# Query-times-kv products in two row tiles of 64 features, over four PSUM banks, and other shares of the banks in each half

## The chip, the cores and the metric

The kernel runs on one core of one Trainium2 chip. The metric is the device time in microseconds (us) of one execution; lower is better. One execution is also recorded by the hardware profiler; all rows below come from it.

The engines are named as in the profile: PE is TensorE (PEld its weight loads), DVE is VectorE, ACT is ScalarE, POOL is GpSimd, SP is the engine that issues most of the DMAs. PE writes to PSUM, which has eight banks of 512 fp32 columns by 128 partitions. Each engine runs its own instructions in order and waits on semaphores for the others.

## The reference

Input x has 2048 rows of 512 features. Two branches work on its normalised form and are added to x:

```python
xn = _layernorm(x, axis=-1)
return x + _A_ref(xn, A_wqkv, A_w_phi, A_wo) + _B_ref(xn, B_w1, B_b1, B_w2)
```

Branch A is linear attention with 32 heads of 16 features. Each head's q and k go through a 16x16 matrix and become two softmaxes of 16, one of p and one of -p:

```python
phi_k = jnp.concatenate([_softmax(pk, axis=-1), _softmax(-pk, axis=-1)], axis=-1)
kv = jnp.einsum("bhsf,bhsd->bhfd", phi_k, v)
z  = jnp.einsum("bhsf->bhf", phi_k)
num = jnp.einsum("bhqf,bhfd->bhqd", phi_q, kv)
den = jnp.einsum("bhqf,bhf->bhq", phi_q, z)[..., None] + 1e-6
o = num / den
```

and o goes through wo. Branch B is a dense layer to 1792 features with bias, Mish, and a dense layer back to 512.

## The kernel before

The 2048 rows are 16 tiles of 128 rows, four tiles to a group. The order of the instructions on every engine is the order in which the code issues them.

**First half** (the loop over s, lines 505 to 542): for each group, project makes logits (p) and values, extremes (DVE) subtracts the largest and smallest of each head, exponentials (ACT) takes Exp, normalise (DVE) divides, and accumulate adds up kv over all rows. Between these, hidden(n) does the next n of 56 units of the dense layer: four matmuls into one PSUM bank (ph), then one Mish on ACT that empties it into acts. Logits and values also go through one bank each, which ACT or DVE empties.

accumulate (line 276) already works in column tiles: its products for 64 features each are put on two halves of PE's columns with tile_position=(0, 64 * r). Its result pkv has eight blocks (two softmaxes pl by four j of eight heads), and mask_kv (line 295) moves them into kvm, keeping only each head's own 16 columns, with the sums z in eight more columns and eight columns of a fixed mask. So a block of kvm is 128 features by 144 columns.

**Second half** (from line 545). exponentials of the query groups 4 to 7 are turned by DMA into qT. attend(h, i) (line 330) multiplies one tile of queries with kvm: eight matmuls of 144 columns, 128 features each, into pnd; four ACT copies move the numerators to nm and the rest to ds. combine(h) (line 359) works for two tiles: DVE makes one divisor out of both softmaxes' sums, multiplies, adds, and a DMA turns the result into oT. second_layer(t) (line 409) opens a bank po and does 14 matmuls of branch B; project_out(h) (line 419) adds four matmuls with wo for each of the tiles 2h and 2h+1, and residual (line 429) adds x on DVE, which empties po, and starts the store.

The loop over h (lines 564 to 590) writes the order out by hand. For h = 1, 3, 4 and 5 it issues combine(h + 1) before project_out(h); for h = 0 and 2 after it, and there four logits follow, and later extremes. Then come attend(h + 2, 0), second_layer(2h + 4), attend(h + 2, 1), second_layer(2h + 5). At h = 5 it issues attend(7, 0), combine(6), combine(7) for its first tile, project_out(5), attend(7, 1) and the second layers of tiles 14 and 15. So when project_out(h) is issued, the po of tiles 2h to 2h + 3 are open. Tile 15 has two po, one for each half of the columns.

**PSUM** is shared out for the whole kernel at the start:

```python
ps = ctx.enter_context(tc.tile_pool(name="ps", bufs=5, space=bass.MemoryType.PSUM))
ps2 = ctx.enter_context(tc.tile_pool(name="ps2", bufs=1, space=bass.MemoryType.PSUM))
```

ps has five banks for all one-bank tiles (pfold, ptr, pproj, ph, po); a new tile takes the bank that has been free the longest, and its first matmul waits until that bank's last reader is done. ps2 is one tile of three banks, which is in turn pwide (three logits at s = 0, lines 516 to 518, emptied by one ACT copy after hidden(6), line 540), pkv and pnd.

Of the kernel before, what the change touches and what calls it, by code (L numbers as in the profile page):

```python
# [1 line left out]

# [15 lines left out]
def kernel(  # L18
# [39 lines left out]
    opool = ctx.enter_context(tc.tile_pool(name="opool", bufs=2))  # L58
    ps = ctx.enter_context(tc.tile_pool(name="ps", bufs=5, space=bass.MemoryType.PSUM))
    ps2 = ctx.enter_context(tc.tile_pool(name="ps2", bufs=1, space=bass.MemoryType.PSUM))  # L60

    x_sb = persist.tile([P, NT, D], BF16, name="x_sb")
    xnT = persist.tile([P, NT, KT, P], BF16, name="xnT")
    acts = persist.tile([P, FT, S], BF16, name="acts")
    kvm = persist.tile([P, 2, 4, 144], BF16, name="kvm")
    wqk = wts.tile([P, KT, 2 * D], BF16, name="wqk")
# [12 lines left out]
    block = consts.tile([P, 8, 16], BF16, name="block")  # L79
    KVmask = consts.tile([P, 136], FP32, name="KVmask")  # L80
    vext = [vpool.tile([P, TPG, 4, 2, 68], BF16, name=f"vext{i}") for i in range(2)]
# [11 lines left out]
    def fold(wT, dst, dve):  # L93

        for kt in range(KT):
            pf = ps.tile([P, 512], FP32, name="pfold", tag="mm")
            for j in range(4):
                nc.tensor.matmul(
                    pf[:, j * P : (j + 1) * P],
                    lhsT=wT[:, j, kt * P : (kt + 1) * P],  # L100
                    rhs=Wbd[:, j, :],
                    start=True,
                    stop=True,
                )
            if kt in dve:
                nc.vector.tensor_copy(dst[:, kt, :], pf[:])
            else:
                nc.scalar.copy(dst[:, kt, :], pf[:])
# [28 lines left out]
    def ln_turn_pe(t, xn, i, copy):  # L137
        ptr = ps.tile([P, 512], BF16, name="ptr", tag="mm")
        for kt in range(KT):
            nc.tensor.transpose(  # L140
                ptr[:, kt * P : (kt + 1) * P], xn[:, i, kt * P : (kt + 1) * P], ident[:]
            )
        copy(xnT[:, t, :, :], ptr[:].rearrange("p (k c) -> p k c", k=KT))
# [7 lines left out]
    def project(w, t, pp=None):  # L151

        if pp is None:
            pp = ps.tile([P, 512], FP32, name="pproj", tag="mm")[:]
        for kt in range(KT):
# [14 lines left out]

    def hidden(n):

        for _ in range(n):
            g, f = next(units)
            ph = ps.tile([P, 512], FP32, name="ph", tag="mm")
            for kt in range(KT):
# [86 lines left out]

    def blocks(kv, pl, j, width):

        bank, at = (pl, j) if j < 3 else (2, pl)
        return kv[:, bank, at * 144 : at * 144 + width]

    def by_parts(kv, c0, c1):

        v = kv[:, :, 0:432].rearrange("p b (k c) -> p b k c", c=144)
        return v[:, 0:2, :, c0:c1], v[:, 2, 0:2, c0:c1]

    kv_of = {}

    def accumulate(g):
        if g == 0:
            kv_of[0] = ps2.tile([P, 3, 512], FP32, name="pkv", tag="kv")
        e = e_of.pop(g)
        for j in range(4):  # L280
            for pl in range(2):
                for i in range(TPG):
                    for r in range(2):
                        c = j * P + 64 * r
                        nc.tensor.matmul(
                            blocks(kv_of[0], pl, j, 65)[64 * r : 64 * r + 64],
                            lhsT=e[:, i, pl, c : c + 64],
                            rhs=vext[g % 2][:, i, j, r, 0:65],
                            start=(g == 0 and i == 0 and (j == 0 or (j == 3 and pl == 0))),
                            stop=(g == NG - 1 and i == TPG - 1),  # L290
# [4 lines left out]
    def mask_kv():  # L295
        for r in range(2):
            rows, c = slice(64 * r, 64 * r + 64), slice(64 * r, 64 * r + 64)
            a, b = by_parts(kv_of[0], 0, 64)
            nc.vector.tensor_tensor(
                out=kvm[rows, :, 0:3, c], in0=a[rows],  # L300
                in1=KVmask[rows, None, None, c].to_broadcast([64, 2, 3, 64]), op=ALU.mult,
            )
            nc.vector.tensor_tensor(
                out=kvm[rows, :, 3, c], in0=b[rows],
                in1=KVmask[rows, None, c].to_broadcast([64, 2, 64]), op=ALU.mult,
            )
        a, b = by_parts(kv_of[0], 64, 65)
        for pl in range(2):
            nc.vector.scalar_tensor_tensor(
                out=kvm[:, pl, 0:3, 128:136], in0=a[:, pl].to_broadcast([P, 3, 8]), scalar=5e-7,  # L310
                in1=KVmask[:, None, 128:136].to_broadcast([P, 3, 8]),
                op0=ALU.add, op1=ALU.mult,
            )
        nc.vector.scalar_tensor_tensor(
            out=kvm[:, :, 3, 128:136], in0=b.to_broadcast([P, 2, 8]), scalar=5e-7,
            in1=KVmask[:, None, 128:136].to_broadcast([P, 2, 8]), op0=ALU.add, op1=ALU.mult,
        )

    def masks():
        nc.gpsimd.memset(kvm[:], 0.0)  # L320
        nc.gpsimd.tensor_copy(KVmask[:, 0:P], block[:].rearrange("p h d -> p (h d)"))
        nc.gpsimd.tensor_copy(KVmask[:, P : P + 8], block[:, :, 0])
        nc.gpsimd.tensor_copy(
            kvm[:].rearrange("p l j c -> p (l j) c")[:, :, 136:144],
            block[:, None, :, 0].to_broadcast([P, 8, 8]),
        )

    nd_of, oT_of, po_of, tmp_of = {}, {}, {}, {}

    def attend(h, i):  # L330

        if i == 0:
            nd_of[h] = (
                (wkp, wv)[h % 2][:].rearrange("p (i l) c -> p i l c", i=2),
                opool.tile([P, 2, 2, 2, 4, 8], FP32, name="ds"),
            )
        nm, ds = nd_of[h]
        pnd = ps2.tile([P, 3, 512], FP32, name="pnd", tag="kv")
        for pl in range(2):
            for j in range(4):  # L340
                nc.tensor.matmul(  # L341
                    blocks(pnd, pl, j, 144),
                    lhsT=qT_of[h][:, i, pl * 4 + j, :],
                    rhs=kvm[:, pl, j, :],
                    start=True,
                    stop=True,
                )
        to = nm[:, i, :, :].rearrange("p l (j c) -> p l j c", j=4)
        a, b = by_parts(pnd, 0, 128)
        nc.scalar.copy(to[:, :, 0:3, :], a)  # L350
        nc.scalar.copy(to[:, :, 3, :], b)
        a, b = by_parts(pnd, 128, 144)
        nc.scalar.copy(
            ds[:, i, :, :, 0:3, :].rearrange("p l x j h -> p l j x h"),
            a.rearrange("p l j (x h) -> p l j x h", x=2),
        )
        nc.scalar.copy(ds[:, i, :, :, 3, :], b.rearrange("p l (x h) -> p l x h", x=2))

    def combine(h, parts=(slice(0, 2),)):

        nm, ds = nd_of.pop(h) if parts[-1].stop == 2 else nd_of[h]
        ds = ds[:].rearrange("p i l x j h -> p i l x (j h)")
        if h not in oT_of:
# [7 lines left out]
        for q in parts:  # L371
            n = q.stop - q.start
            nc.vector.tensor_tensor(
                out=u[:, q], in0=ds[:, q, :, 0, :], in1=ds[:, q, ::-1, 1, :], op=ALU.mult
            )
            nc.vector.tensor_tensor(
                out=w[:, q], in0=u[:, q, 0, :], in1=u[:, q, 1, :], op=ALU.add
            )
            nc.vector.reciprocal(w[:, q], w[:, q])
            nc.vector.tensor_tensor(  # L380
                out=u[:, q], in0=ds[:, q, ::-1, 1, :],
                in1=w[:, q, None, :].to_broadcast([P, n, 2, 32]), op=ALU.mult,
            )
            nc.vector.tensor_copy(
# [24 lines left out]
    def second_layer(t, f0=0, f1=FT):  # L409
        if f0 == 0:  # L410
            po_of[t] = [ps.tile([P, 512], FP32, name="po", tag="mm") for _ in halves(t)]
        for po, c in zip(po_of[t], halves(t)):
# [47 lines left out]

    warm = ps.tile([P, 4, P], FP32, name="warm", tag="mm")
    for _ in range(12):
        nc.tensor.matmul(  # L463
            warm[:], lhsT=ident[:], rhs=ident[:, None, :].to_broadcast([P, 4, P]),
            start=True, stop=True,
        )
# [13 lines left out]
    ln_turn_pe(1, xn, 1, act)  # L480
    pb = ps.tile([P, 512], BF16, name="pb", tag="mm")
    nc.tensor.transpose(pb[:, 0:FT], b1b[:], ident[0:FT, 0:FT])
# [22 lines left out]
    for s in range(NG):  # L505
# [6 lines left out]
        if s == 0:  # L512
            p_of[1] = smx.tile([P, TPG, 512], BF16, name="p_sb", bufs=1)
            act(p_of[1][:, 0, :], project(wkp, TPG))
            exponentials(0, (1,))
            wide = ps2.tile([P, 3, 512], FP32, name="pwide", tag="kv")
            for i in range(3):
                project(wkp, TPG + 1 + i, wide[:, i, :])
        else:
# [18 lines left out]
        if s == 0:  # L538
            hidden(6)
            act(p_of[1][:, 1:4, :], wide[:])  # L540
        hidden((11, 14, 8, 10)[s])
# [6 lines left out]
    for i in range(TPG):  # L548
        logits(5, i, act if i == 3 else dve)
    second_layer(0)  # L550
    hidden(2)
# [12 lines left out]
    for h in range(2 * NG):  # L564
# [17 lines left out]
        if h == 5:  # L582
            attend(7, 1)
        for i in range(2):
            if t < NT:
# [35 lines left out]
```

## Time and profile before

| what | value |
|---|---|
| median of three runs | 182.84 us (182.77 to 182.93) |
| the profiled execution | 182.85 us |
| its span, first to last instruction | 181.1 us |
| PE matmul over the span | 173.9 us in 1152 instructions |
| matmuls of attend (L341) | 128, 0.50 us for each eight |
| matmuls of accumulate (L285) | 256 |
| ACT copies of pnd (L350, L351, L353, L357) | 0.80, 0.38, 0.26, 0.22 us each |
| mask_kv on DVE | 97.45 to 99.34 us |
| mean granted TensorE clock | 0.999 |

A row of the timeline reads: start in us from the first instruction, time from the first start to the last end in us, engine, line, operation, what it writes and reads, shape, count; in brackets the idle time of the engine before it and what ended that. Matmuls overlap in the pipeline: a wide one (512 columns) is listed with 0.38 us, but one starts every 0.216. A row of the chain of waits reads: start, length, engine and line.

### The profile page before, as it was taken

How to read it: one execution, taken by the hardware profiler on the slowest of the kernel's cores; microseconds unless marked ns; L12 is line 12 of the kernel's file. 1: busy time of each engine (PE TensorE's matmuls, PEld its weight loads, DVE VectorE, ACT ScalarE, POOL GpSimd, SP SyncE). 2: the span in 40 equal slices, each digit the busy share in tenths (PEclk: the TensorE clock that was granted, in tenths of full speed). 3: DMA queues.
4: the chain of work that ended last, by engine and by line, in shares of the span. 5: the costliest groups of instructions: out<-in, count | busy, mean ns of one | idle time of the engine just before them, and what ended most of it. 6: DMA issues, size and time to landing. Idle time of an engine off the chain costs nothing.

```text
span 181.1 us, 3005 instructions
## 1 busy us (share of the span) xinstructions
PE 173.9 (96%) x1152; PEld 87.0 (48%) x1167; DVE 146.3 (81%) x254; ACT 126.2 (70%) x194; POOL 26.8 (15%) x34
## 2 busy tenths in 40 slices
PE   6899999999999999998999999999999999999992
PEld 2454344454444545543454545455554545455561
DVE  1989979997999989988999895399917997637963
ACT  2367999999998899969986989472942567235200
POOL 4404069400797000000000000000000000000000
PEclk9999999999999999999999999999999999999999
DMA  6998896300023900000000791953089302990533
GB/s 146 294 390 279 158 346 179 70 1 5 0 58 63 114 0 0 4 0 0 4 0 0 148 87 23 188 136 63 0 177 207 79 5 47 200 192 26 86 91 116
DMA packets 44394, 18.04 MB, mean 100 GB/s; under 512 B 36828, under 2 KB 43868, under 8 KB 44380
## 3 DMA queue, kind: packets, MB, share of 16 engines
q1 hardware_dynamic: 43408, 17.50, 42.8%
q10 hardware_dynamic: 972, 0.35, 0.7%
q8 instruction: 9, 0.15, 0.4%
q14 instruction: 5, 0.04, 0.1%
HBM read 6.84 MB, written 2.10 MB: 49 GB/s over the span
## 4 chain that ended last, share of the span: by engine, by line
PE 50%; DVE 38%; ACT 4%; DMA 4%; issue 2%; POOL 0%; DVEq 0%; POOLq 0%
PE po L414 20%; PE ph L177 8%; DVE s L247 7%; PE po L423 7%; DVE m L208 7%; DVE e L219 5%; PE pproj L156 5%; DVE e L260 4%; ACT e L229 4%; PE pnd L341 3%; DVE r L255 3%; PE warm L463 3%; DVE stats L116 3%; DMA xnT<-xn 2%; DMA ob<-ob 2%
## 5 line engine op out<-in xcount | busy, mean ns | idle before, releaser
L414 PE MATMUL po<-w_sb,acts 128*128 128x512 bf16 (+1 forms) x232 | 50.3, 366 | 0.3
L177 PE MATMUL ph<-xnT,w_sb 128*128 128x512 bf16 x224 | 49.5, 379 | 0.1
L184 ACT ACTIVATE acts<-ph,b1f 128x512 bf16<-128x512 f32 x56 | 35.1, 703 | 2.5 <-PE ph L177 2.3
L177 PEld LDWEIGHTS <-w_sb 128*128 128x128 bf16 x224 | 21.9, 98 | 26.6 <-issue 0.5
L229 ACT ACTIVATE e<-e 128x2048 bf16<-128x2048 bf16 x16 | 29.8, 1903 | 6.9 <-DVE e L219 6.9
L414 PEld LDWEIGHTS <-acts 128*128 128x128 bf16 x238 | 22.8, 98 | 22.0
L156 PEld LDWEIGHTS <-xnT 128*128 128x128 bf16 x192 | 18.2, 98 | 23.0 <-DMA xnT<-xn 1.1
L247 DVE TENSOR_REDUCE s<-e 128x128 f32<-128x2048 bf16 x8 | 18.2, 2277 | 2.6 <-ACT e L229 2.6
L195 ACT CAST p_sb<-pproj 128x512 bf16<-128x512 f32 x25 | 13.7, 587 | 9.4 <-PE pproj L156 9.4
L431 DVE TENSOR_TENSOR x_sb<-po,x_sb 128x512 bf16<-128x512 f32 (+1 forms) x17 | 10.6, 654 | 11.4 <-PE po L423 11.4
L128 POOL TENSOR_SCALAR xn<-x_sb,mv,rstd 128x512 bf16<-128x512 bf16 x8 | 16.7, 2101 | 0.2
L156 PE MATMUL pproj<-wv,xnT 128*128 128x512 bf16 x61 | 15.0, 379 | 0.9 <-ACT p_sb L195 0.8
L423 PE MATMUL po<-wqk,ob 128*128 128x512 bf16 (+1 forms) x66 | 14.7, 366 | 0.3 <-DMA ob<-ob 0.2
L156 PE MATMUL pproj<-wqk,xnT 128*128 128x512 bf16 x62 | 14.4, 379 | 0.1
L350 ACT CAST wkp<-pnd 128x768 bf16<-128x768 f32 x8 | 6.4, 799 | 11.2 <-PE pnd L341 7.3
L116 DVE BATCH_NORM_STATS2 stats<-x_sb 128x6 f32<-128x512 bf16 x16 | 10.0, 679 | 3.8 <-DMA x_sb<-in_A_x_dram 3.8
L208 DVE TENSOR_TENSOR m<-m 128x512 bf16<-128x512 bf16 (+1 forms) x32 | 11.6, 363 | 1.1
L156 PE MATMUL pproj<-wkp,xnT 128*128 128x512 bf16 x50 | 11.8, 379 | 0.1
L208 DVE TENSOR_TENSOR m<-p_sb 128x1024 bf16<-128x1024 bf16 x16 | 11.0, 684 | 0.7 <-ACT p_sb L195 0.7
L341 PEld LDWEIGHTS <-qT 128*128 128x128 bf16 x128 | 9.1, 98 | 3.9 <-issue 0.3
L341 PE MATMUL pnd<-kvm,qT 128*128 128x144 bf16 x128 | 10.6, 226 | 0.0
L350 ACT CAST wv<-pnd 128x768 bf16<-128x768 f32 x8 | 6.3, 792 | 5.9 <-PE pnd L341 3.7
(68 smaller groups left out, 174.8 us busy)
## 6 DMA issues: line engine op xcount, KB each, us to landing
w_sb<-in_B_w_dram SPq DMA_DIRECT2D x2, 1792.0 KB, 9.1
out_dram<-x_sb SPq DMA_DIRECT2D x15, 128.0 KB, 1.8
x_sb<-in_A_x_dram SPq DMA_DIRECT2D x1, 1024.0 KB, 11.8
x_sb<-in_A_x_dram SPq DMA_DIRECT2D x1, 512.0 KB, 4.1
wv<-in_A_wqkv_dram SPq DMA_DIRECT2D x1, 512.0 KB, 4.9
wqk<-in_A_wo_dram SPq DMA_DIRECT2D x1, 512.0 KB
x_sb<-in_A_x_dram SPq DMA_DIRECT2D x1, 256.0 KB, 2.9
x_sb<-in_A_x_dram ACTq DMA_DIRECT2D x1, 256.0 KB, 3.5
```

The lines of the kernel that those rows point to most:

```text
L116: nc.vector.bn_stats(stats[:, i, :], x_sb[:, t0 + i, :])
L128: engine.tensor_scalar(out=xn[:, at + i, :], in0=x_sb[:, t0 + i, :], scalar1=mv[:, i, 0:1], scalar2=rstd[:, i : i + 1], op0=ALU.subtract, ...
L156: nc.tensor.matmul(pp, lhsT=xnT[:, t, kt, :], rhs=w[:, kt, :], start=(kt == 0), stop=(kt == KT - 1),)
L177: nc.tensor.matmul(ph[:], lhsT=w1_sb[:, kt, f * P : (f + 1) * P], rhs=xnT[:, g * TPG : (g + 1) * TPG, kt, :], start=(kt == 0), stop=(kt == ...
L184: nc.scalar.activation(acts[:, f, g * 512 : (g + 1) * 512], ph[:], ACT.Mish, bias=b1f[:, f : f + 1])
L195: copy(p_of[s][:, i, :], pp)
L208: nc.vector.tensor_tensor(out=m[:], in0=src[:, :, 0:half], in1=src[:, :, half : 2 * half], op=op)
L229: nc.scalar.activation(v, v, ACT.Exp)
L247: nc.vector.reduce_sum(t[:], v.rearrange("p t l (c e) -> p (t l c) e", e=16), axis=AX.X)
L341: nc.tensor.matmul(blocks(pnd, pl, j, 144), lhsT=qT_of[h][:, i, pl * 4 + j, :], rhs=kvm[:, pl, j, :], start=True, stop=True,)
L414: nc.tensor.matmul(po[:, c], lhsT=acts[:, f, t * P : (t + 1) * P], rhs=w2_sb[:, f, c], start=(f == 0), stop=False,)
L423: nc.tensor.matmul(po[:, c], lhsT=oT_of[h][:, t % 2 * 4 + j, :], rhs=wo_sb[:, j, c], start=False, stop=(j == 3),)
```

## The change

The products of queries with kv are split by rows. kvm keeps, for each block, only 64 columns of numerators, four of sums and four of the mask, for each half of 64 features (72 columns instead of 144). attend does 16 matmuls of 64 features by 72 columns, in pairs on the two halves of PE's rows, and each half writes to banks of its own, so pnd has four banks. ACT moves them out with two copies. ds has another order, and combine's two operations that read it are issued once for each of the two tiles.

pkv has two banks. In the first half the other six serve all one-bank tiles, four as ps and two as px, taken in a fixed turn; at s = 0 the three logits sit in pearly, two in px and one in ps, and hidden(6) takes ps alone. Before second_layer(0), px and pk close and their four banks become pnd. In the second half ps with four banks serves all else; after attend(7, 1) pnd's banks are given up and one bank is opened for the second po of tile 15.

```diff
-    ps = ctx.enter_context(tc.tile_pool(name="ps", bufs=5, space=bass.MemoryType.PSUM))
-    ps2 = ctx.enter_context(tc.tile_pool(name="ps2", bufs=1, space=bass.MemoryType.PSUM))
+    ps = ctx.enter_context(tc.tile_pool(name="ps", bufs=4, space=PSUM))
+    upper = ExitStack()
+    px = upper.enter_context(tc.tile_pool(name="px", bufs=2, space=PSUM))
+    pk = upper.enter_context(tc.tile_pool(name="pk", bufs=1, space=PSUM))
+    later = []
+    turns = cycle([ps, px, ps, ps, px, ps])
+
+    def bank(name, dtype=FP32, pool=None):
+        pool = pool or (ps if later else next(turns))
+        return pool.tile([P, 512], dtype, name=name, tag="x" if pool is px else "mm")
...
-    def hidden(n):
+    def hidden(n, pool=None):
...
-            ph = ps.tile([P, 512], FP32, name="ph", tag="mm")
+            ph = bank("ph", FP32, pool)
...
     def mask_kv():
...
+        kv = kv_of[0][:, :, 0:260].rearrange("p l (j c) -> p l j c", j=4)
+        nc.vector.tensor_tensor(
+            out=kvm[:, :, :, 0:64], in0=kv[:, :, :, 0:64],
+            in1=KVmask[:, None, None, 0:64].to_broadcast([P, 2, 4, 64]), op=ALU.mult,
+        )
         for pl in range(2):
             nc.vector.scalar_tensor_tensor(
...
+                out=kvm[:, pl, :, 64:68], in0=kv[:, pl, :, 64:65].to_broadcast([P, 4, 4]),
+                scalar=5e-7, in1=KVmask[:, None, 64:68].to_broadcast([P, 4, 4]),
                 op0=ALU.add, op1=ALU.mult,
             )
...
     def masks():
-        nc.gpsimd.memset(kvm[:], 0.0)
...
+        for r in range(2):
+            rows, own = slice(64 * r, 64 * r + 64), block[64 * r : 64 * r + 64, 4 * r : 4 * r + 4, :]
+            nc.gpsimd.tensor_copy(KVmask[rows, 0:64], own.rearrange("p h d -> p (h d)"))
+            nc.gpsimd.tensor_copy(KVmask[rows, 64:68], own[:, :, 0])
+            nc.gpsimd.tensor_copy(
+                kvm[rows].rearrange("p l j c -> p (l j) c")[:, :, 68:72],
+                own[:, None, :, 0].to_broadcast([64, 8, 4]),
+            )
...
-        pnd = ps2.tile([P, 3, 512], FP32, name="pnd", tag="kv")
+        pnd = later[0].tile([P, 4, 512], FP32, name="pnd", tag="nd")
         for pl in range(2):
             for j in range(4):
-                nc.tensor.matmul(
-                    blocks(pnd, pl, j, 144),
-                    lhsT=qT_of[h][:, i, pl * 4 + j, :],
-                    rhs=kvm[:, pl, j, :],
-                    start=True,
-                    stop=True,
-                )
...
+                for r in range(2):
+                    rows = slice(64 * r, 64 * r + 64)
+                    nc.tensor.matmul(
+                        pnd[:, 2 * r + pl, j * 72 : j * 72 + 72],
+                        lhsT=qT_of[h][rows, i, pl * 4 + j, :],
+                        rhs=kvm[rows, pl, j, :],
+                        start=True,
+                        stop=True,
+                        tile_position=(64 * r, 0),
+                    )
+        a = pnd[:, :, 0:288].rearrange("p (r l) (j c) -> p r l j c", r=2, j=4)
+        to = nm[:, i, :, :].rearrange("p l (j r c) -> p r l j c", j=4, r=2)
+        nc.scalar.copy(to, a[:, :, :, :, 0:64])
+        nc.scalar.copy(ds[:, i].rearrange("p l j r c -> p r l j c"), a[:, :, :, :, 64:72])
...
-            nc.vector.tensor_tensor(
-                out=u[:, q], in0=ds[:, q, :, 0, :], in1=ds[:, q, ::-1, 1, :], op=ALU.mult
-            )
...
+            for i in range(n):
+                k = q.start + i
+                nc.vector.tensor_tensor(
+                    out=uh[:, i], in0=ds[:, k, :, 0], in1=ds[:, k, ::-1, 1], op=ALU.mult
+                )
...
-            po_of[t] = [ps.tile([P, 512], FP32, name="po", tag="mm") for _ in halves(t)]
+            po_of[t] = [
+                bank("po", FP32, later[1] if c.stop == 512 and c.start else None)
+                for c in halves(t)
+            ]
...
-            wide = ps2.tile([P, 3, 512], FP32, name="pwide", tag="kv")
+            early = [bank("pearly", FP32, p) for p in (px, px, ps)]
             for i in range(3):
-                project(wkp, TPG + 1 + i, wide[:, i, :])
+                project(wkp, TPG + 1 + i, early[i][:])
...
-            hidden(6)
-            act(p_of[1][:, 1:4, :], wide[:])
+            hidden(6, ps)
+            for i in range(3):
+                act(p_of[1][:, 1 + i, :], early[i][:])
+            early = None
         hidden((11, 14, 8, 10)[s])
...
+    upper.close()
+    after = ExitStack()
+    later.append(after.enter_context(tc.tile_pool(name="pq", bufs=1, space=PSUM)))
     second_layer(0)
...
             attend(7, 1)
+            after.close()
+            later.append(ctx.enter_context(tc.tile_pool(name="pe", bufs=1, space=PSUM)))
```

## The prediction

> **What bounds the kernel now.** The profiled execution took 182.85 us, of which 181.1 are the span and 1.7 lie around it; the median of the three runs is 182.84, so the sum is made against 182.85. I read the page first, then the chain of waits in order of time, then the timeline at each place where the change moves a bank.
>
> ```profile
> PE 173.9 (96%) x1152; PEld 87.0 (48%) x1167; DVE 146.3 (81%) x254; ACT 126.2 (70%) x194; POOL 26.8 (15%) x34
> ...
> PE 50%; DVE 38%; ACT 4%; DMA 4%; issue 2%; POOL 0%; DVEq 0%; POOLq 0%
> ```
>
> PE is nearly always busy, yet the chain is half DVE: two engines are full, and they take turns. By order of time the chain is on PE until 42 us, then passes through DVE (with some Exp on ACT) until 111.5 us, over one DMA, and stays on PE to the end:
>
> ```profile
> 111.53 3.18 DMA ob<-ob
> 114.71 0.05 issue
> 114.76 1.90 PE po L423 x8
> ```
>
> So PE time gained between 42 and 114.76 us is worth nothing: the first project_out waits for DVE's combine(0). A delay of PE before 42 us, or after 114.76, counts in full.
>
> **Part 1, the tiled products.** Before, an attend is 8 matmuls of 144 columns in 0.50 us (128.72 to 129.22 in the fence on the loop below), 62.5 ns each. After, it is 16 of 72 columns and 64 rows. The trace shows no row tiles; the nearest row is accumulate, which has column tiles:
>
> ```profile
> 39.65 1.20 PE L285 MATMUL pkv<-vext,e 128*64 128x65 bf16 x64
> ...
> 40.79 1.90 PE L156 MATMUL pproj<-wv,xnT 128*128 128x512 bf16 x7
> 41.86 0.69 DVE L164 CAST vext<-pproj 128x512 bf16<-128x512 f32 x1 [1.38 <-PE pproj L156]
> ```
>
> In its single records two matmuls start together, and the pairs follow every 32 ns. But the change of mode costs: the last matmul before it starts at 39.34, the first pair at 39.65 (0.31 where 0.216 is usual), and the next wide one 0.13 after the last pair; with a slow first pair that is 0.22 us for going in and out. Eight pairs of 72 columns: 8 x 32.5 ns + 0.22 = 0.48 us against 0.50. I take no gain. Bounds: 0.26 if row tiles change mode for nothing; 0.74 if the pairs don't overlap (16 x 32.5 + 0.22); 1.2 if each 128-column weight load takes the 62.5 ns that loads take in the old attend.
> The Trainium skill, TensorEngine Tiling (Array Packing), section Theoretical Speedup, gives up to 2x for a dimension of at most 64. By that alone the sixteen attends would give back 16 x 0.25 = 4 us of PE time; the trace's 0.22 us for the two switches takes nearly all of it.
>
> **Part 2, six banks in the first half.** The one long bank wait there is 0.8 us for "ACT p_sb L195" at 84.25; six banks remove it, but in the stretch where DVE leads: 0. At 7.9 us a transpose waited 0.6 us for the bank that L106 empties; its own copy waits for ACT until 8.80 anyway (it ran at 9.07), so -0.1 (from -0.6 to 0).
>
> **Part 3, hidden(6) on three banks.** Before, these six units turn through five banks while the wide tile holds three others. After, pearly holds both px banks and one of the four ps, and hidden(6, ps) has three.
>
> ```profile
> 24.72 9.60 PE L177 MATMUL ph<-xnT,w_sb 128*128 128x512 bf16 x43
> ...
> 27.17 1.28 ACT L184 ACT_TABLE_LOAD   x1
> ...
> 28.46 3.58 ACT L184 ACTIVATE acts<-ph,b1f 128x512 bf16<-128x512 f32 x6
> ```
>
> ACT empties the first unit only at 29.15, behind an Exp and a table load. A unit takes PE 0.864, so the fourth starts at 27.31 now; with three banks it starts at 29.20. The sixth, at 29.20 today, moves to 30.93: +1.73. The second unit of the next call falls on px and wants it at 32.65; ACT copies the first pearly behind the sixth Mish, until about 33.2: +0.55. Together +2.28. DVE sits idle 1.38 us at 41.86, waiting for exactly this PE work, so nothing absorbs it, and all that follows moves by 2.3.
>
> **Part 4, small work on DVE, ACT and POOL.** mask_kv falls from seven DVE operations in 1.9 us (97.45 to 99.34) to three, about 0.9 by the 0.68 of a 128x512 copy from PSUM; DVE waits 0.65 us for ACT's last p_sb at 101.78 right behind, so 0; without that wait the 1.0 would be a gain. combine gets two more operations of 64 elements (0.22 each, against 0.29 for the one of 128). They don't depend on each other, so most of a second hides in the first: +0.06 each, +0.12 per combine; bound 0.36 if nothing hides. combine(0) is on the path: +0.1. ACT's four copies per attend take 1.31 us, two take about 1.2 (1.01 by the slope from 256 to 768 elements, plus 0.28 less overlap): -0.1. The masks on POOL run before 80 us; POOL is idle from then on: 0. po15b's own bank opens when ACT has copied attend(7,1), at 169.8; its matmuls come after 171.2: 0.
>
> **Part 5, four banks in the loop.** When project_out(h) ends, tiles 2h to 2h+3 hold four po. Now the fifth ps bank takes po of tile 2h+4 at once. After, that po needs the bank of tile 2h, which residual frees; and for h = 1, 3, 4, 5 combine is issued ahead of project_out, so residual queues on DVE behind it.
>
> ```profile
> 129.22 3.19 PE L414 MATMUL po<-w_sb,acts 128*128 128x512 bf16 x13
> 130.00 0.69 DVE L398 TENSOR_TENSOR ob<-wkp 128x1024 bf16<-128x1024 bf16 x1
> 130.62 1.28 DVE L431 TENSOR_TENSOR x_sb<-po,x_sb 128x512 bf16<-128x512 f32 x2
> ```
>
> Here, h = 1, po of tile 6 starts at 129.22, while the first residual ends at 131.30. With 0.05 for the semaphore (29.15 to 29.20 above) and two combines at +0.12: 131.30 + 0.05 + 0.24 - 129.22 = 2.37. The other three:
>
> ```profile
> 158.97 1.28 DVE L431 TENSOR_TENSOR x_sb<-po,x_sb 128x512 bf16<-128x512 f32 x2
> 158.98 1.89 PE L414 MATMUL po<-w_sb,acts 128*128 128x512 bf16 x8
> ...
> 168.25 3.73 PE L414 MATMUL po<-w_sb,acts 128*128 128x512 bf16 x19
> ...
> 170.25 1.28 DVE L431 TENSOR_TENSOR x_sb<-po,x_sb 128x512 bf16<-128x512 f32 x2
> ```
>
> h = 3: po starts at 150.21, the first residual ends at 152.29: 2.37 likewise. h = 4: 159.65 + 0.05 + 0.12 - 0.1 (ACT, whose copies combine(5) waits for) - 158.98 = 0.74. h = 5: 170.93 + 0.05 + 0.02 - 168.25 = 2.75. Each wait moves all of PE behind it, and with it the logits and attends from which DVE starts the next round, so they add up. Of the attends only (0,1), (3,1), (5,1) and (6,1) still lie on the path; the rest run while DVE is awaited. h = 0 and 2 have residual ahead of combine: nothing.
>
> **Sum.** -0.1 + 2.28 + 0.1 + 2.37 + 2.37 + 0.74 + 2.75 = 10.5 us; 182.85 + 10.5 = **193.4 us**, span 191.7. Its own range: with combine at the upper bound seven times (+1.7) 195.1; without the px wait and with the full 0.6 at the start 192.3.
>
> **Rivals.**
> A. The pauses of 2.4 to 2.75 us slow the TensorE clock. At the end of the trace PE stops at 177.96, and the granted clock in the window 180 to 181.1 is 0.94, so it fell some 3.0 us after the last matmul: close. The start shows the price: twelve matmuls at 0.427 us instead of 0.216 before the rate doubles, 2.5 us for one fall. One fall gives 195.9, three 200.9. Chance 0.12.
> The Trainium skill, TensorE: Matmul & The Clock Gate, Part 1, has an idle window of about 3.4 us before the clock halves. By that rule none of these pauses is long enough and this rival costs nothing; the 3.0 us in the trace is shorter than the rule's window.
> B. Row tiles don't overlap, or their weight loads take turns. An attend is 0.74 to 1.2 us, four on the path: +1.0 to +2.9, 194.4 to 196.3. For it: no row tile is in the trace. Against: column tiles pair well. Chance 0.10.
> C. The delay in the first half is caught up before 114.76, so that only the loop pays: 191.1. For it: PE loses a bank wait at 84. Against: DVE leads there without a gap that PE could fill. Chance 0.08.
> D. The other side: PE alone sets the loop and no po waits, as no po waits today. The twelve attends after 114.76 give 12 x 0.24 = 2.9 us: 180. That needs switches for nothing, the early delay absorbed, and a free bank at po of tile 6; it decides from the point where that po follows attend(3,0) without a gap. Against: four po live in four banks. Chance 0.04, a quarter of it landing within the noise.
>
> **Numbers.** Forecast 0.66, A 0.12, B 0.10, C 0.08, D 0.04. The range 190.9 to 198.0 holds forecast, C, B and one fall of the clock; beyond it lie D and several falls. About 0.2% (0.4 us) is what a measurement of this kernel can tell from no change: faster 0.03, same 0.01, slower 0.96.
>
> **What would show it.** Waits of PE's "po L414" for "DVE x_sb L431" (their lines will have moved), four of them, 0.7 to 2.8 us; a wait of "ph" for ACT of 1.9 us near 27; the first project_out near 117; attends near 0.5 us each, from their first matmul to the next wide one; a granted clock of 1.0 through all pauses. The prediction is wrong if po of tile 6 starts at once, or if project_out(0) starts near 115.

## The result, and the profile after

The changed kernel takes 198.47 us (median of four runs, 198.44 to 199.97), beside 182.88 (182.77 to 183.11) for the kernel before in the same session: a ratio of 1.0871 [1.0847, 1.0895]. The prediction was 193.4 with a range up to 198.0; the time lies 0.47 above the range. The profiled execution took 198.47, with a span of 196.8, so 1.7 lie around the span as before. A run more than 1.5% above the fastest of its kernel counts as slow and is left out of the ratios given here, which concerns two of the six runs of experiment 8 and no other. The page of the profiled execution:

```profile
PE 178.6 (91%) x1295; PEld 83.8 (43%) x1295; DVE 146.3 (74%) x264; ACT 124.6 (63%) x164; POOL 27.0 (14%) x36
...
PEclk9999999999999999999999999996999969999699
...
DVE 59%; PE 25%; ACT 7%; issue 3%; DMA 3%; DVEq 0%
```

Two things are new. In the chain of waits DVE has 59% where it had 38, and PE has 25 where it had 50: PE no longer runs to the end by itself but waits for DVE. And the row of the granted clock has three slices of 6, which begin at 133, 157 and 182 us. The waits of PE for a bank, from the view of waits (engine, tile and line, releaser: us in total, times, longest):

```profile
PE po L411 <- DVE x_sb L428: 7.7, 4, 2.5
...
PE ph L187 <- ACT acts L194: 1.3, 1, 1.3
...
PE ph L187 <- ACT p_sb L538: 0.4, 1, 0.4
```

All three were in the forecast: po waits for residual (four times, of which three take 2.3 to 2.5 us), hidden(6) waits for Mish, and the unit after it for the copy of pearly. The first pause of the loop, in the timeline:

```profile
130.54 0.43 PE L333 MATMUL pnd<-kvm,qT 64*128 64x72 bf16 x16
...
130.72 1.23 DVE L385 TENSOR_TENSOR wkp<-wkp,f 128x2048 bf16<-128x2048 bf16 x1
...
131.98 0.69 DVE L392 TENSOR_TENSOR ob<-wkp 128x1024 bf16<-128x1024 bf16 x1
...
132.59 1.28 DVE L428 TENSOR_TENSOR x_sb<-po,x_sb 128x512 bf16<-128x512 f32 x2
...
133.32 1.02 PE L411 MATMUL po<-w_sb,acts 128*128 128x512 bf16 x4 [2.35 <-DVE x_sb L428]
```

attend(3, 0) is done at 130.97. DVE is inside combine(2) for another 1.6 us, then does the first residual (132.59 to 133.27), and 0.05 after it po of tile 6 starts. The step that the forecast put at 2.37 is here: PE stands idle for 2.35. Measured from the start of attend(3, 0), po starts 2.28 later than in the kernel before, where it follows at once.

What the forecast did not have stands in the table by stretches of the same trace (stretch, its length, busy time and count of PE, PEld, DVE, ACT, POOL, then the granted clock, the DMA share and GB/s). The stretches are 3.41 us long and come in pairs, each pair cut where the clock changes:

```profile
131.09:134.50 3.41, 1.18 (x6) 0.58 (x6) 2.74 (x4) 2.56 (x3) 0.00 (x0) 1.00 0.20 45
134.50:137.91 3.41, 3.41 (x10) 1.06 (x7) 0.00 (x0) 0.00 (x0) 0.00 (x0) 0.50 0.83 194
154.98:158.39 3.41, 1.07 (x20) 0.50 (x18) 3.27 (x8) 3.41 (x3) 0.00 (x0) 1.00 0.00 0
158.39:161.80 3.41, 3.40 (x9) 1.17 (x9) 0.68 (x2) 0.33 (x2) 0.00 (x0) 0.50 0.69 176
178.87:182.28 3.41, 1.22 (x6) 0.58 (x6) 3.18 (x9) 0.90 (x2) 0.00 (x0) 1.00 1.17 97
182.28:185.69 3.41, 3.41 (x10) 1.21 (x8) 1.64 (x5) 0.00 (x0) 0.00 (x0) 0.50 0.47 130
```

Three times the clock is at 0.50 for one stretch of 3.41 us, and each time the stretch just before it has PE busy for only 1.07 to 1.22 us. In the slow stretch a wide matmul starts every 0.427 us instead of every 0.216; eight of them fit in, and 8 x 0.211 = 1.7 us are lost.

The starts of the same matmuls in both traces, and what each step adds (us):

| where | before | after | shift | added by |
|---|---|---|---|---|
| accumulate(0), first | 39.65 | 41.65 | +2.00 | hidden(6) on three banks |
| project_out(0), first | 114.76 | 116.44 | +1.68 | transposes of ob 2.72 instead of 3.18: -0.46; combine(0) |
| po of tile 6 | 129.22 | 133.32 | +4.10 | bank 2.28 |
| po of tile 10 | 150.21 | 158.40 | +8.19 | clock 1.81, bank 2.28 |
| po of tile 12 | 158.98 | 169.31 | +10.33 | clock 1.73, bank 0.41 |
| po of tile 14 | 168.25 | 181.06 | +12.81 | bank 2.44 |
| end of the last matmul | 177.96 | 192.45 | +14.49 | clock 1.68 |
| the last store has landed | 180.05 | 195.66 | +15.61 | the last store 1.12 |

A bank's entry is how much later po starts after the attend in front of it than in the kernel before; a clock's entry is what is added from that po to the next attend on the path, or to the end. The last store lands 2.67 us after its issue (192.99 to 195.66), 1.55 before (178.50 to 180.05). The view of DMA (what is moved, issuing queue, count, size, us to landing), first before, then after:

```profile
out_dram<-x_sb SPq DMA_DIRECT2D x1, 64.0 KB, 1.5
```

```profile
out_dram<-x_sb SPq DMA_DIRECT2D x1, 64.0 KB, 2.7
```

So of 15.6 us the banks in the loop are 7.4, the clock 5.2, the first half 1.7 at the place where it counts, and the last store 1.1; the remaining 0.2 lies between these places.

### The profile page after: what moved, and what is told of

It is laid out like the page before. It is cut to its first block, busy times and chain, and to the rows that moved or that the text cites. A ratio compares the mean times of both kernels' runs of the same rounds, so it can differ in the third digit from the quotient of the medians.

```text
span 196.8 us, 3259 instructions
## 1 busy us (share of the span) xinstructions
PE 178.6 (91%) x1295; PEld 83.8 (43%) x1295; DVE 146.3 (74%) x264; ACT 124.6 (63%) x164; POOL 27.0 (14%) x36
## 4 chain that ended last, share of the span: by engine, by line
DVE 59%; PE 25%; ACT 7%; issue 3%; DMA 3%; DVEq 0%
PE po L411 13%; DVE m L218 10%; DVE e L229 8%; DVE s L257 7%; PE ph L187 6%; ACT e L239 5%; DVE stats L126 5%; DVE e L270 4%; PE po L420 3%; DVE r L265 3%; DVE ob L392 3%; DVE wkp L385 3%; DVE x_sb L428 2%; DVE wv L385 2%; DVE w L372 2%
## 5 line engine op out<-in xcount | busy, mean ns | idle before, releaser
L411 PE MATMUL po<-w_sb,acts 128*128 128x512 bf16 (+1 forms) x238 | 56.0, 393 | 7.7 <-DVE x_sb L428 7.7
L411 PEld LDWEIGHTS <-acts 128*128 128x128 bf16 x238 | 23.6, 103 | 34.0 <-issue 14.0
L343 ACT CAST wv<-pnd 128x1024 bf16<-128x1024 f32 x8 | 8.0, 1004 | 14.2 <-PE pnd L333 11.9
L343 ACT CAST wkp<-pnd 128x1024 bf16<-128x1024 f32 x8 | 8.1, 1014 | 11.8 <-PE pnd L333 7.7
L218 DVE TENSOR_TENSOR m<-m 128x512 bf16<-128x512 bf16 (+1 forms) x32 | 11.5, 360 | 1.1
L270 DVE TENSOR_TENSOR e<-e,r 128x2048 bf16<-128x2048 bf16 x8 | 10.2, 1281 | 0.3
L366 DVE TENSOR_TENSOR u<-ds 128x64 f32<-128x64 f32 x16 | 3.1, 219 | 9.8 <-ACT ds L344 9.8
```

Of the source, the lines that this page charges most:

```text
L218: nc.vector.tensor_tensor(out=m[:], in0=src[:, :, 0:half], in1=src[:, :, half : 2 * half], op=op)
L270: nc.vector.tensor_tensor(out=vv, in0=vv, in1=r2[:, :, None, :].to_broadcast([P, 128, 8, 2]), op=ALU.mult)
L343: nc.scalar.copy(to, a[:, :, :, :, 0:64])
L411: nc.tensor.matmul(po[:, c], lhsT=acts[:, f, t * P : (t + 1) * P], rhs=w2_sb[:, f, c], start=(f == 0), stop=False,)
```

## The experiments

Theory: two shortages of banks make the loss of PE time (hidden(6) on three banks, four banks for po), the pauses in the loop make the clock fall, and the row tiles themselves cost nothing. Rival: the row tiles or the new mode of PE cost time of their own, or the clock has another cause. All kernels are the changed kernel with the edit shown, unless another is named. Experiments 1 to 4 ran once each, the others four times or more.

**1. The residual that frees the bank, run inside combine.** For h = 1, 3 and 4 project_out leaves its residuals in a list; the first is issued inside combine(h + 1), behind the copy to f, the second behind it.

```diff
-        if h in (1, 3, 4, 5):
-            combine(h + 1)
-        if h == 5:
-            combine(7, first)
...
-        project_out(h)
+        left = [] if h in (1, 3, 4, 5) else None
+        project_out(h, left)
+        if h in (1, 3, 4):
+            combine(h + 1, between=lambda: residual(*left[0]))
+            residual(*left[1])
+        if h == 5:
+            combine(6)
+            for x in left:
+                residual(*x)
+            combine(7, first)
```

> The changed kernel, but for h = 1, 3 and 4 the residual of tile 2h runs inside combine(h + 1), behind its copy to f, and at h = 5 both residuals run ahead of combine(7). Theory (the loop waits for a bank that residual frees too late, and the long waits make the TensorE clock fall): the four waits of 2.28, 2.27, 0.41 and 2.44 us shrink to 0.4 or less each, the clock stays at 1.0 (5.2 us back), so 186 to 187 us. Rival (the row tiles or the longer combine slow the loop, and the waits only show it): the loop keeps most of its length and the time stays above 193.

Measured: 186.94 (the kernel before beside it 182.84), mean clock 0.999. The timeline at the place of the first pause:

```profile
131.14 0.68 DVE L433 TENSOR_TENSOR x_sb<-po,x_sb 128x512 bf16<-128x512 f32 x1
131.74 1.22 DVE L387 TENSOR_TENSOR wkp<-wkp,f 128x2048 bf16<-128x2048 bf16 x1
...
131.88 1.46 PE L413 MATMUL po<-w_sb,acts 128*128 128x512 bf16 x6 [0.35 <-DVE x_sb L433]
```

The residual now stands ahead of the 1.22 us multiplication instead of behind it, and 2.35 us of waiting become 0.35. All po waits together are 0.7 us, the clock stays up, and 11.5 us are back. Moving residual in DVE's order shows both at once: the long bank waits come from residual's place in DVE's queue, and without them there is no fall.

**2. project_out before combine, for every h.**

```diff
-        if h in (1, 3, 4, 5):
-            combine(h + 1)
...
         project_out(h)
-        if h in (0, 2):
+        if h < 6:
             combine(h + 1)
```

> The changed kernel with project_out(h), and so both residuals, issued ahead of combine(h + 1) for every h. Theory: no wait for a bank and no fall of the clock, but combine ends 2 to 3 us later and its DMA lands 0.3 to 1 us after project_out needs it at h = 2, 4, 6 and 7: 187 to 189 us. Rival (bank waits are not the cause): above 193.

Measured: 189.99, mean clock 0.996. No po waits for residual any more, but PE stands still six times for the transpose of ob, 4.4 us in all and 1.3 at the longest, since combine now begins later. The direction is right; the time is 1 to 3 us above what was expected. Combine ahead of project_out had brought oT in time.

**3. hidden(6) on five banks.** At s = 0 two of the early logits go into the two banks of pk, which wait for pkv anyway; hidden(6) takes all of px and ps that are free.

```diff
-            early = [bank("pearly", FP32, p) for p in (px, px, ps)]
+            two = pk.tile([P, 2, 512], FP32, name="ptwo", tag="kv")
+            early = [two[:, 0, :], two[:, 1, :], bank("pearly", FP32, ps)]
...
-            hidden(6, ps)
+            hidden(6)
```

> The changed kernel with two of the three early logits in the two kv banks, which are unused at that time, so that hidden(6) turns through five banks (three of ps, two of px). Theory (the delay before accumulate(0) goes to the end in full): PE's wait of 1.3 us and the one of 0.4 us near 29 to 33 us are gone, accumulate(0) starts near 39.5 instead of 41.65, and the time falls by 1.6 to 2.2 to 196.3 to 196.9. Rival (DVE's chain absorbs it): 198.5 as before. If the places of the waits against the clock's steps matter, a fall of the clock may come or go besides, 1.7 us each.

Measured: 193.29, some 3 us less than expected. The first half does as expected: accumulate(0) starts at 39.85 instead of 41.65, the first project_out at 114.63, and ph no longer waits for Mish. The rest, 3.4 us, is the clock, which fell twice less. The pauses are the same as in the changed kernel (2.35, 2.35 and 2.51 us), yet only one fall follows; the stretches are cut as above:

```profile
128.56:131.97 3.41, 1.06 (x21) 0.62 (x20) 3.32 (x5) 3.28 (x4) 0.00 (x0) 1.00 0.00 0
131.97:135.38 3.41, 3.41 (x10) 1.22 (x9) 0.09 (x1) 0.00 (x0) 0.00 (x0) 0.50 0.84 205
152.45:155.86 3.41, 1.79 (x23) 0.86 (x22) 3.24 (x8) 3.41 (x3) 0.00 (x0) 1.00 0.00 0
155.86:159.27 3.41, 2.68 (x12) 1.26 (x13) 1.41 (x4) 1.06 (x2) 0.00 (x0) 1.00 0.58 153
172.93:176.34 3.41, 2.04 (x23) 0.99 (x23) 3.21 (x8) 2.36 (x4) 0.00 (x0) 1.00 0.79 43
176.34:179.75 3.41, 2.17 (x11) 0.98 (x11) 3.15 (x10) 0.00 (x0) 0.00 (x0) 1.00 0.47 114
```

The second and third pause each lie across a boundary: PE is busy 1.79 and 2.04 us in one stretch, 2.68 and 2.17 in the next. The first lies within one stretch, with 1.06. So a fall seems to need the pause inside one of the steps, whose boundaries come every 3.413 us and do not follow the kernel.

**4. Zero products in the pauses.** For h = 1, 3 and 5 PE adds ten products with a tile of zeros to the po that is open, in the time in which it would wait.

```diff
+                if i == 0 and h in (1, 3, 5):
+                    for _ in range(10):
+                        nc.tensor.matmul(
+                            po_of[2 * h + 2][0][:], lhsT=zero[:], rhs=w2_sb[:, 0, :],
+                            start=False, stop=False,
+                        )
                 second_layer(t + i)
```

> The changed kernel with ten matmuls of a zero tile added to an open po at h = 1, 3 and 5, just ahead of the po that waits for its bank. They add zeros and fill 2.16 of the 2.35 to 2.5 us in which PE stands idle; the waits for the bank stay. Theory (the pause makes the granted clock fall for 3.4 us, which costs 1.7 us each time): clock 1.0 and 193.3 us. Rival (the falls in the clock rows cost nothing, the loop is slow by itself): 198.5 or more.

Measured: 193.71, mean clock 1.0. The bank comes as late as before, PE only does useless work until then, and 198.47 - 193.71 = 4.8 us are gone with the three falls. This is the price of the clock by itself (5.2 by the table above; here the first project_out also starts 0.3 later than in the changed kernel).

**5. The kernel before, with four banks in the second half.** No row tiles, no other layout; the fifth bank is kept for the second po of tile 15.

```diff
-    ps = ctx.enter_context(tc.tile_pool(name="ps", bufs=5, space=bass.MemoryType.PSUM))
+    ps = ctx.enter_context(tc.tile_pool(name="ps", bufs=4, space=bass.MemoryType.PSUM))
+    px = ctx.enter_context(tc.tile_pool(name="px", bufs=1, space=bass.MemoryType.PSUM))
...
+            po_of[t] = [
+                bank("po", FP32, px if c.stop == 512 and c.start else None) for c in halves(t)
+            ]
```

> The kernel before, with its own attend, kvm and combine, but from second_layer(0) on with four banks for all one-bank tiles; its fifth bank takes the second po of tile 15 only. Theory (the shortage of banks alone makes the loop slow, not the row tiles): po of tiles 6, 10, 12 and 14 waits for residual by 2.1, 2.1, 0.7 and 2.7 us, 190.5 us with no fall of the clock, 1.7 more for each fall, up to 195.6. Rival (the row tiles, the order of ds or the longer combine do it): 182.9 as before.

Measured: 192.61 (192.18 to 192.72), ratio 1.0521 [1.05, 1.0542]. Its view of waits, and its stretches around the second and the fourth pause:

```profile
PE po L424 <- DVE x_sb L441: 6.9, 4, 2.6
```

```profile
151.74:155.15 3.41, 1.53 (x14) 0.93 (x13) 3.34 (x5) 3.41 (x6) 0.00 (x0) 1.00 0.00 0
172.22:175.63 3.41, 1.35 (x12) 0.83 (x11) 3.11 (x10) 1.82 (x8) 0.00 (x0) 1.00 0.48 48
175.63:179.04 3.41, 2.89 (x7) 1.02 (x7) 3.20 (x9) 0.00 (x0) 0.00 (x0) 0.50 0.58 149
```

The same four waits, 6.9 us in all, and one fall: 190.5 + 1.7 = 192.2, as expected of one. Row tiles are not needed for the loss in the loop; a bank less is enough. The stretches also narrow the limit of the clock: 1.53 us of work in a step kept it up, 1.35 did not. The second pause, 1.88 us long (152.77 to 154.65), lies wholly inside its step and cost nothing but itself.

**6. Both cures.** Experiments 1 and 3 together; the first residual now stands ahead of the copy to f.

```diff
+            if between is not None:
+                between()
             nc.vector.tensor_copy(
                 f[:, q].rearrange("p i l c o -> p (i l c) o"),
```

> The changed kernel with both cures: residual of tile 2h inside combine (now ahead of its copy to f), and two early logits in the kv banks. Theory: 186.94 of the first cure, less 2.3 for the first half and 0.6 for the rest of the waits: 183.6 to 184.4, clock at 1.0 up to the last matmul, and what is left above the kernel before is the last store (2.65 us to land instead of 1.55) against 0.04 us saved per attend. Rival (the tiled products cost more than their own time): above 185.

Measured: 184.13 (183.95 to 184.18), ratio 1.0059 [1.0037, 1.008]. PE no longer waits for a bank for more than 0.4 us anywhere, and the last matmul ends at 177.99, where the kernel before has 177.96. What remains lies behind it: the last store takes 2.82 us instead of 1.55.

**7. The same with twelve more instructions on ACT.** In the trace of the changed kernel a packet of 8 KB of a queue for instructions (q14) runs at 194.43 for 0.45 us, in the middle of the last store, and the last nine packets of the store start only behind it, from 194.88 on; in the kernel before the last packet of this queue comes at 163.1. ACT's program is 29 instructions shorter after the change, so the reading is that its next block of code is fetched later. Twelve one-column copies into a new tile, at h = 4, where ACT is idle, should bring the fetch forward.

```diff
+        if h == 4:
+            for k in range(12):
+                nc.scalar.copy(spare[:, k : k + 1], mhalf[:, 0:1])
```

> The same as e6 with twelve copies of one column on ACT at h = 4, where ACT is idle. Theory on the last store (a fetch of 8 KB of instructions, queued on one of the DMA engines just as the store runs, delays its last packets; it comes when ACT has used up a piece of its program): the fetch moves to an earlier place, the store lands after 1.55 us, and the time is 1.1 us below e6, about 182.9. Rival (the fetch is another engine's, or the store is late for another reason): as e6, 183.6 to 184.4.

Measured: 183.43 (183.25 to 183.62), ratio 1.0026 [1.0015, 1.0036]. The fetch moved from 179.6 to 151.9, and the last store takes 1.54 us. But about half of the 1.3 us went elsewhere: PE waits 1.0 us for the transposes of ob, whose median is 3.1 us here and 2.7 in experiment 6.

**8. Experiment 3 once more, six runs.**

> The kernel of e3 once more, run several times. It had the three long pauses of the changed kernel (2.3, 2.3 and 2.5 us) but one fall of the clock instead of three. Theory (the clock looks at steps of 3.41 us that run freely against the kernel, and a pause counts if about 2.1 us or more of it lie in one step): its times differ from run to run by steps of 1.7 us, 191.6, 193.3, 195.0 or 196.7. Rival (the place of each pause in the kernel decides): all runs at 193.3.

| time, us | 191.57 | 191.73 | 192.19 | 193.12 | 196.31 | 197.0 |
|---|---|---|---|---|---|---|
| mean clock | 1.0 | 0.995 | 1.0 | 0.987 | 0.971 | 0.971 |

One step of 3.41 us at half clock takes 0.009 off the mean of a span of 191 us, and a little more is lost when the fall after the last matmul still lies in the span. By that the runs at 1.0 and 0.995 have no fall in the loop and those at 0.971 three; only the run of 193.12 was traced, and it has one. So one program with the same pauses falls to half clock a different number of times from run to run, as it must if the steps run freely and each execution lies differently in them. This holds by the runs up to 193.12 alone, whose ratio to the kernel before is 1.05 [1.0469, 1.0531]; with the two longest the distance from no fall to three is 197.0 - 191.6 = 5.4 us, 1.8 each. So 198.47 is no fixed sum either: one of the four runs of the changed kernel took 199.97, at a mean clock of 0.963 instead of 0.972.

**9. One row tile after the other.** Experiment 6 with r as the outer loop: eight products of the first 64 features, then eight of the second.

```diff
-        for pl in range(2):
-            for j in range(4):
-                for r in range(2):
+        for r in range(2):
+            for pl in range(2):
+                for j in range(4):
```

> The kernel of e6 with the order of the sixteen matmuls changed: the eight of the lower 64 features first, then the eight of the upper, so that no two neighbours are on different row tiles. Theory (an attend is short only because neighbours on two row tiles run together): the sixteen take 0.52 us or more instead of 0.27, twelve attends after the first project_out count, so 3 us or more above e6: 187 us. Rival (weight loads or the two changes of mode set the price of an attend, not the overlap): as e6, 184.1.

Measured: 185.3 (185.2 to 185.68), ratio 1.0137 [1.0123, 1.0151]. Two rows of PE's timeline, the first of experiment 6, the second of this kernel:

```profile
141.03 0.43 PE L333 MATMUL pnd<-kvm,qT 64*128 64x72 bf16 x16
```

```profile
141.75 0.58 PE L333 MATMUL pnd<-kvm,qT 64*128 64x72 bf16 x16
```

An attend is 0.15 us longer; from its first matmul to the next wide one 0.51 instead of 0.37. Over twelve attends that is 1.7 us, and with a last store 0.5 shorter (2.3 us) 184.13 + 1.7 - 0.5 = 185.3. So the pairing in the change is real, but its loss had been expected at 3 us. The two tiles overlap partly even where neighbours do not alternate: in the single records the second tile's products start 0.15 us after the first's, while those of the first go on until 0.235.

**10 and 11. Five copies on ACT, with and without a new tile.** In experiment 7 the new tile also moved what lies behind it in memory. Five copies go once into a new tile and once into KVmask, which is no longer needed by then.

```diff
+        if h == 4:
+            for k in range(5):
+                nc.scalar.copy(KVmask[:, k : k + 1], mhalf[:, 0:1])
```

> The kernel of e6 with five copies of one column on ACT at h = 4 instead of twelve, so that the fetch of instructions falls neither on the last store nor on the DMA of a combine that project_out is about to need. Theory: the last store lands after about 1.6 us, no wait of 0.8 us for ob at 157, and the time is 182.6 to 183.0, no longer above the kernel before. Rival (the fetch costs about as much wherever it falls): 183.4 as e7.

> The kernel of e10, but its five copies on ACT write into KVmask, which is no longer read by then, so that no tile is added and all other tiles lie where they lie in e6. In e10 and e7 the added tile moved ob by 64 bytes, and the DMA transposes of ob took 3.05 to 3.2 us instead of the 2.73 of e6. Theory (the fetch costs e6 1.1 us at its last store; the moved tile cost e10 0.3 to 0.7 us elsewhere): last store 1.55 us, first transposes 2.73, 182.7 to 183.1. Rival (the fetch costs as much wherever it falls): 183.4 or more.

Measured: 183.73 (183.46 to 183.9), ratio 1.0047 [1.0035, 1.0059] with the new tile, 182.85 (182.55 to 183.15), ratio 0.9995 [0.9984, 1.0005] without. Experiment 10 missed what was expected of it and lies nearer to its rival, experiment 11 lies where it was expected. Both have a last store of 1.5 us. They differ in ob, from the view of DMA (what is moved, issuing queue, count, median us to landing), first with the new tile, then without:

```profile
ob<-ob SPq DMA_TRANSPOSE x9, 3.1
```

```profile
ob<-ob SPq DMA_TRANSPOSE x9, 2.7
```

In the compiled program with the new tile ob begins at byte 155200 of a partition, without it, as in the changed kernel, at 155136, a multiple of 512 and of 256. In the kernel before it begins at 156544, a multiple of neither, and its transposes take 3.1 too. The expectations speak of 512; experiment 4, where ob begins at 155392 (607 x 256) and its transposes take 2.7, shows that 256 is enough. So the -0.46 in the table of shifts has nothing to do with the change's purpose: tiles ahead of ob became smaller (KVmask and kvm are the ones that the diff shrinks), and ob slid to another place.

**12. The kernel before, with ob moved.** An unused tile of 128 bytes ahead of KVmask.

```diff
+    pad = consts.tile([P, 32], FP32, name="pad")
     KVmask = consts.tile([P, 136], FP32, name="KVmask")
```

> The kernel before with an unused tile of 128 bytes per partition, so that ob begins at a multiple of 512 bytes as in the changed kernel. Theory (the place of the tile sets the length of the DMA transposes of ob): they take 2.73 us instead of 3.1, the first project_out starts 0.3 to 0.4 us earlier, and the time is 182.4 to 182.6. Rival (the length comes with the other changes, such as the order of ds or the banks): transposes of 3.1 us, 182.9 as before.

Measured: 182.44 (182.27 to 182.86), ratio 0.9973 [0.9964, 0.9983]; ob begins at 156672 (612 x 256), its transposes take 2.7 us, and the first project_out starts at 114.20 instead of 114.76. This beats the kernel before, by 0.27%, and the changed kernel with every cure: experiment 11, with ob at a multiple of 256 too, is 0.4 us slower. From the first project_out to the end of the last matmul the two take 63.2 and 63.3 us, so the few hundredths that an attend saves do not show in the loop. One difference in the traces: the two longest transposes of ob take 4.2 and 4.6 us in experiment 11 and the longest 3.6 in experiment 12. In all fourteen traces a transpose of ob above 3.3 us is one during which a packet of 16 KB of another queue for instructions (q8) starts. Whether that makes the 0.4 us is not shown.

The Trainium skill, DMA: Bandwidth & Descriptors, section How a descriptor splits into AXI transactions, has a rule for how a descriptor, the order for one piece of a transfer, is split: each transaction must start at a multiple of 256 bytes, so a descriptor that starts elsewhere begins at the multiple below it and fetches bytes that it does not use. The starts tried here go with it (medians of 2.7 us at the three multiples of 256, 3.0 to 3.1 at the two others); no run here shows the transactions themselves, nor that the rule is the reason for a transpose.

## Why the prediction was wrong, point by point

**The step that failed** is the rule by which the forecast left the clock alone. It took three pauses of 2.37 to 2.75 us as too short for a fall and put that into rival A with a chance of 0.12. Of the signs that it named, the four waits of po, the wait of ph, the first project_out near 117 and the attends near 0.5 us came more or less as said; the granted clock of 1.0 through all pauses did not. The runs show that the length of a pause does not decide by itself, but how much of it lies inside one step of 3.41 us: a step in which PE works 1.35 us or less is followed by one at half clock, and a pause of 2.35 us inside one step is enough. Whether the sum of the work in a step counts or its longest idle part cannot be told apart here, since each of these steps holds one long pause. Three falls came, 5.2 us by the trace, 4.8 by experiment 4. The evidence that the forecast had, a fall 3.0 us after the last matmul, could not set the limit: the end of work and the end of a step are different times, and the delay between them depends on where the step began. It is 2.0 us in the trace of experiment 5 (187.26 to 189.28) and 3.8 in that of experiment 1 (180.94 to 184.76). Rival A's price was also off: 1.7 us for a fall, not 2.5. The twelve slow matmuls at the start had no full clock before them, while a fall in the loop lasts exactly one step and meets eight.

By the Trainium skill, TensorE: Matmul & The Clock Gate, Part 1, the window of some 3.4 us is free-running. That agrees: 3.413 us in every slow stretch, and a number of falls that differs between runs of one program. The rule drawn from it there, no idle gaps above about 3.4 us, is too lax here: 2.35 us cost a fall.

**The size of the rest.** Without the clock and the last store the sum was 10.5 us, and 1.7 + 7.4 + 0.2 = 9.3 came.
- hidden(6): 2.28 forecast. accumulate(0) is 2.00 later, and experiment 3 puts 1.80 of that down to the banks. It varies from run to run: in the traces with three banks accumulate(0) starts between 41.65 and 42.21, in all others between 39.48 and 40.04. The waits are at the forecast places, for Mish 1.30 and for pearly 0.39.
- combine(0), +0.1 forecast. In experiment 3 the first project_out starts at 114.63, 0.13 earlier than in the kernel before: 0.20 from the later accumulate(0), minus 0.46 for ob, leave 0.13 for all the rest, combine(0) among it; this agrees, though combine(0) was not taken by itself. The gain at ob was not foreseen.
- Bank waits 2.37, 2.37, 0.74 and 2.75 forecast; the shifts are 2.28, 2.28, 0.41 and 2.44. Mechanism and place were right four times, the sum of 8.2 was 0.8 too high.
- Attends at no gain: 0.46 us with the change of mode (0.095 to go in, 0.366 to the next wide matmul) instead of 0.50; the working had 0.48. The pairs follow every 33 ns. Taking no gain was right to 0.04 us, and experiment 9 shows that the overlap is there.
- The last store, +1.1, was in no part: the experiments put it down to ACT's code, not to the data.

**Rivals.** A came, three times, with 1.7 instead of 2.5: 193.4 + 3 x 1.7 = 198.5, which is the time measured only because the store's 1.1 makes up for what the forecast had too much. That the time left the range also hung on the number of falls: one fall less gives 196.8, inside the range, with the same wrong step. B is out: in the changed kernel the pairs overlap and an attend takes 0.46 us. C is out: 1.68 of 2.00 reach the first project_out, and ob explains the rest. D is out: four po waited, and even with these waits removed experiment 11 only equals the kernel before.

That the fetch of ACT's code delays the last store rests on the packet's place in the traces and on three kernels in which more instructions on ACT made the store short again. In the eight traces in which such a packet falls into the last store, it takes 2.3 to 2.8 us, in the six others 1.54 to 1.55; it was not isolated further. In every kernel here the transposes of ob are shorter where ob starts at a multiple of 256 bytes, but other tiles moved with it each time.

## What to carry to other kernels

A bank taken from a pool is priced at the place where its next user waits: find the operation that frees it in the queue of its engine, and move that operation ahead of the long one before the pool is made smaller. A pause of PE cost more than itself, by some 1.7 us, where 2.0 us or more of it lay inside one step of the clock; one of 1.9 did not. So count the work of PE in every 3.4 us, not only the length of the pause, and expect the time to vary from run to run. Where the gain of an edit is a fraction of a microsecond, look at what it shifts without meaning to, the addresses of later tiles and the length of a program, before its effect is put down to the edit.

## What the runs showed of the hardware

- The clock of TensorE is decided in free-running steps of 3.413 us: with PE busy 1.35 us or less in a step the next ran at 0.50, with 1.53 or more it did not. A fall cost 1.7 us of wide matmuls.
- With a packet of a queue for instructions (8 KB, 0.45 us) in its way a store of 64 KB took 2.7 us instead of 1.5; its last nine packets started behind that one.
- DMA transposes of ob took 2.7 us where ob began at a multiple of 256 bytes (three starts) and 3.0 to 3.1 at two other starts, by the medians.
- Two row tiles of 72 columns give a pair every 33 ns, one matmul in 16 ns on average; the change of mode cost about 95 ns in and as much out.
